# Attention and MLP on one core: where split rows live, when turned maxima are sent, and where the MLPs begin

## The chip, the cores and the metric

The kernel runs on one core of one Trainium2 chip. The metric is the time of one execution on the device in microseconds (us). A core has five engines that each work through a queue of their own in order: PE (matmul), DVE (vector), ACT (activation), POOL (general vector work) and SP, which here issues nearly all DMAs. They wait for each other through semaphores.

## The reference, cut to what matters

```python
# x: 2048 x 512; 32 heads of 16; F = 1792
qkv = layernorm(x) @ wqkv                    # q, k, v per head
p   = softmax(q @ k.T / 4)                   # per head, 2048 x 2048
h   = x + (p @ v, heads side by side) @ wo
out = h + silu(layernorm(h) @ w1) @ w2
```

## The kernel before

**Items and groups.** The attention is cut into 32 items of four heads by 512 query rows. Eight items make a block of 512 rows. An item has 16 groups, one for each 128 keys; group g belongs to item g // 16 and has place c = g % 16 in it, so there are 512 groups. In a group PE forms four scores tiles (`scores`: 64 rows of weights, because a head's 16 dimensions stand three times, as parts of a split number, beside 16 rows of constants and maxima), ACT takes the exponential of each (`pt<-ps`), and PE multiplies the weights of the group two before by the values (`values`, `LAG = 2`; in the trace eight matmuls `ps<-pt,va` for one group, since fp32 runs in two passes).

**Maxima.** Softmax subtracts each row's maximum, so for every item 64 further tiles of scores are formed ahead of it (`maximum`: a matmul `ps<-ks,qs` of 48 rows on PE and a reduction `mx<-ps` on DVE). The two kinds use opposite halves of PE's rows, so that a score and a maximum can run at the same time. `maxima(g)` is the planner: it says how many maxima group g takes, from the goals (`AHEAD`: how many groups before an item its maxima should be there) and from a list of `fixed` groups. `at["done"]` counts them.

When the last of an item's 64 maxima is there (`found_maxima`), they are reduced to one number per row and split (`finish_max`: one reduction on DVE and three small operations on POOL if urgent, otherwise nine small operations on POOL), and must stand in two rows of the tile `qs` before the item's first group. There are two ways. If there is time (more than `FAR` groups), `place_far` turns them on DVE (`mt<-ns`) `CALM` steps later, and one and two steps after that SP writes them to DRAM (`md<-mt`) and reads them back (`qs<-md`). If there is little time, `place_max` turns them on PE (`ps<-ident_h,ns`) `WAIT` steps later, DVE copies them (`mn<-ps`), and SP sends them (`qs<-mn`). One step is one group.

**Output and MLP of a block.** While the first item of the next block runs (items 8, 16 and 24, the constant `FIRSTS`), the block's rows are finished. Four tiles of 128 rows (t = 0 to 3): `split_rows` splits the attention's result into two f16 parts (tile `oh`, two buffers); in the groups c = 9 to 12 `output` runs the product with wo, 12 full matmuls each, and amid each product the number of maxima that `MORE` gives; DVE adds x and takes the statistics, `normalize` follows one group later, `split_normal` one more (ACT casts the high part, POOL or DVE subtracts; tile `g`, two buffers), and `turn_beside` transposes it by DMA into `hts` (`hts<-g`). From two groups after the first item, at the groups 146, 274 and 402, `beside_products` runs the MLP amid the attention, six half-matmuls in each group: first `first_of` (hidden units, `end_first` puts them into the tile `gates`), then `second_of`. Those groups are the set `beside`; I call the others plain.

**What sets the order.** The order on each engine is the order in which the code issues; `tick` runs what `soon` has put on the agenda for this step, before the group itself. Every item's accumulator is copied out by `finish_item` (`pvs<-ps`, on DVE for the first eight items and on ACT after).

Of the kernel before, what the change touches and what calls it, by code (L numbers as in the profile page):

```python
# [10 lines left out]
F32 = mybir.dt.float32  # L11
F32R = mybir.dt.float32r
F16 = mybir.dt.float16
# [7 lines left out]
P = 128  # L21
# [5 lines left out]
DC = D // P  # L27
FC = F // P
NB = S // 512
NG = 2 * D // P  # L30
KC = S // P
# [20 lines left out]
RING = 5  # L52
# [11 lines left out]
WAIT = 2  # L64
AHEAD = 6

JOINT = 2
MORE = 3, 3, 0, 0
FAR = 5
CALM = 3  # L70


OUTPUT = 8
# [1 line left out]
LOOK = 5  # L75

LEAD = 5


BESIDE_V = [(0, 0), (0, 0, 4, 4)], [(2, 4), (4, 4, 4, 4)], [(6, 6), (6, 6, 6, 6)]  # L80
# [9 lines left out]
def attention_mlp_kernel(ctx: ExitStack, tc: tile.TileContext, x, wqkv, wo, w1, w2, out):  # L90
# [35 lines left out]
    def dma(*a):  # L126
        pin(nc.sync.dma_start(*a))  # L127
# [157 lines left out]
    def start_of(piece):  # L285
        i, a = piece
        return KC * i + HALF * (a or 0)
# [26 lines left out]
    def finish_max(piece, urgent):  # L314

        m4 = mx.pop(piece).rearrange("p j a q k -> p (j a q) k")
        rows = m4.shape[1]
        nm = small.tile([P, 16], F32, name="nm")[:, :rows]
        sign = 1.0
        if urgent:  # L320
            pin(nc.vector.tensor_reduce(nm, m4, axis=AX.X, op=ALU.max, negate=True))
# [45 lines left out]
    def place_max(piece):  # L367

        i, a = piece
        ns = split.pop(piece)  # L370
        n = ns.shape[1]
        ps = bank("sm", F16)
        tr(ps[:n, :P], ns, ident_h)
        mt = small.tile([32, P], F16, name="mn", bufs=1)[:n]
        dve("tensor_copy", mt, ps[:n, :P])
        for j in range(2):
            dst = qs[i % RING][64 * j + 48:64 * j + 50, slice(None) if a is None else slice(a, a + 1)]
            dst = dst.rearrange("r a n -> r (a n)").rearrange("r (a b) -> r a b", b=P)
            dma(dst, mt[n // 2 * j:n // 2 * (j + 1), :])
        placed.add(piece)  # L380


    todo = {(i, j): sorted(((i, kb, qt, a, j) for kb in range(4) for a in range(2) for qt in range(4)),
# [6 lines left out]
    def soon(steps, fn, *a):  # L390

        agenda.setdefault(at["step"] + steps, []).append((fn, a))
# [15 lines left out]

    def found_maxima(piece):
        g = at["group"]  # L410
        if g is None or piece[1] is None and start_of(piece) - g > FAR:
            soon(WAIT + 1 if g is None else CALM, place_far, piece)
            finish_max(piece, False)
            return
        late.setdefault(at["step"] + WAIT, []).append(piece)
        unfinished.append(piece)
        found_at["step"] = at["step"]

# [43 lines left out]
    def weave(steps, inserts):  # L462

        for k, _ in enumerate(steps):
            if k + 1 in inserts:
# [4 lines left out]
    pts, den = {}, {}  # L470
    marks = [KC * (8 * b + 1) for b in range(1, NB)]

    beside = {g for m in marks for g in range(m + 2, min(groups, m + 2 + 4 * FC + 4 * FC))}
    fixed = {**{8 * KC * b + c: 3 + (MORE[c - OUTPUT - 1] if OUTPUT < c <= OUTPUT + 4 else 0) for b in range(1, NB) for c in range(2, KC + 2)},
             **{g: 4 for g in beside}}
    before = [sum(n for x, n in fixed.items() if x < g) for g in range(groups + 1)]
    free = [sum(x not in fixed for x in range(g)) for g in range(groups + 1)]
# [530 lines left out]
    def parts_of(w):  # L1008
        return w.bitcast(F16).rearrange("p (s n) -> p s n", s=2)
# [26 lines left out]

    def split_rows(b, t, chunks=slice(None)):
        if chunks.start != DC - 1:
            parts = zp.tile([P, 2, DC, P], F16, name="oh")
            os[t] = parts[:, 0], parts[:, 1]  # L1040
        (h, l), o = (x[:, chunks] for x in os[t]), ot[b % 2][:, t, chunks]
        if t > 1:
            act("copy", h, o)
        else:

            pool("tensor_copy", h, o)
        low(l, o, h, "pool")
# [26 lines left out]
    halves = {}  # L1074

    def split_normal(t):
        rows, halves[t] = hx.pop(t), parts_of(zp.tile([P, 512], F32, name="g"))
        act("copy", halves[t][:, 0], rows)
        low(halves[t][:, 1], rows, halves[t][:, 0], "pool" if t < 3 else "dve")

# [96 lines left out]

    def begin_mlp(b):
        chains.extend((3 * DC, 6, first_of(f), lambda ps, f=f: end_first(f, ps)) for f in range(FC))
        chains.extend((3 * FC, 7 if 4 * b + t == KC - 5 else 6, second_of(t), lambda ps, t=t: end_second(b, t, ps)) for t in range(4))  # L1180

    def half_product(j):
        if j == 0:
# [187 lines left out]
    def maxima(g):  # L1371

        i, c = divmod(g, KC)
        ready = at["ready"] = min(ITEMS, i + RING - (0 if c == KC - 1 else 1)) * 64
        late_now = at["step"] in late
        if g in beside:
            at["due"] = 0
            most = 4 - late_now + (64 + 4 * (g + (LEAD if g < marks[-1] else 3)) > at["done"])
            return max(0, min(most, ready - at["done"]))
        goals = [(64 * (n + 1), KC * n) for n in range(i + 1, LAST) if g >= FIRSTS[0] * KC or n <= FIRSTS[0] + 1]  # L1380
        goals += [(END - 32 * (1 - a), KC * LAST + HALF * a) for a in range(2) if g >= FIRSTS[0] * KC and KC * LAST + HALF * a > g]
        rate = 0
        for n, start in goals:
            end = max(g + 1, start - AHEAD)
            rate = max(rate, (n - (before[end] - before[g]) - at["done"]) / max(1, free[end] - free[g]))
        if g in fixed:
            rate = 3
        if ready < END:
            rate = min(rate, (ready - at["done"]) / (KC - 1 - c or KC))
        at["due"] += rate  # L1390
        if g < LAG:
            at["due"] = 0
            return 0
        most = 2 if late_now or c == JOINT and 0 < i <= FIRSTS[0] else 3 + (at["due"] >= 4 and i < FIRSTS[0])
# [116 lines left out]
```

## Time and profile before

| | us |
|---|---|
| median of 3 runs (1584.95 to 1586.16) | 1585.84 |
| the profiled execution | 1586.9 |
| its span on the core | 1585.1 |
| PE busy | 1561.1 |
| DVE busy | 1376.3 |
| ACT busy | 1234.7 |
| POOL busy | 573.6 |

The page says that the ends of matmuls are modelled, so that a busy PE is not PE at its peak: two matmuls on opposite halves of the rows count once, and so does one that runs alone. Stages are therefore compared by the time from one group's first value product to the next one's, with the granted clock (PEclk) beside it. The time outside the span is 1.8 us.

### The profile page before, as it was taken

How to read it: one execution, taken by the hardware profiler on the slowest of the kernel's cores; microseconds unless marked ns; L12 is line 12 of the kernel's file. 1: busy time of each engine (PE TensorE's matmuls, PEld its weight loads, DVE VectorE, ACT ScalarE, POOL GpSimd, SP SyncE). 2: the span in 40 equal slices, each digit the busy share in tenths (PEclk: the TensorE clock that was granted, in tenths of full speed). 3: DMA queues.
4: the chain of work that ended last, by engine and by line, in shares of the span. 5: the costliest groups of instructions: out<-in, count | busy, mean ns of one | idle time of the engine just before them, and what ended most of it. 6: DMA issues, size and time to landing. Idle time of an engine off the chain costs nothing.

```text
span 1585.1 us, 31197 instructions
## 1 busy us (share of the span) xinstructions
PE 1561.1 (98%) x11488; PEld 502.2 (32%) x11488; DVE 1376.3 (87%) x2202; ACT 1234.7 (78%) x2404; POOL 573.6 (36%) x843
## 2 busy tenths in 40 slices
PE   9999999999999999999999999999999999999999
PEld 6433222222222333333322333333322333332354
DVE  7999999999998999999988999999988999994322
ACT  6545799999977888888877888888867888878632
POOL 6643545454432545212242454302242445211100
PEclk9999999999999999999999999999999999999999
DMA  6667523334334122344433211444433221334332
GB/s 217 171 177 224 138 83 90 90 108 115 85 92 98 47 51 53 105 137 135 124 84 82 58 44 48 122 130 131 115 96 75 60 57 38 85 119 147 106 87 73
DMA packets 135554, 162.47 MB, mean 102 GB/s; under 512 B 42512, under 2 KB 79440, under 8 KB 135400
## 3 DMA queue, kind: packets, MB, share of 16 engines
q1 hardware_dynamic: 130648, 151.95, 34.6%
q10 hardware_dynamic: 4752, 8.52, 1.9%
q8 instruction: 90, 1.47, 0.4%
q14 instruction: 64, 0.52, 0.1%
HBM read 126.66 MB, written 24.81 MB: 96 GB/s over the span
## 4 chain that ended last, share of the span: by engine, by line
PE 84%; DVE 8%; ACT 3%; issue 1%; POOL 1%; DMA 1%; SPq 0%; ACTq 0%; POOLq 0%; DVEq 0%
PE ps L97 84%; DVE mx L307 5%; ACT pt L111 2%; DVE mx L305 1%; PE ps L100 1%; DMA hts<-g 0%; SPq L127 0%; ACT pvs L111 0%; DVE st L121 0%; POOL rs L104 0%; DMA ks<-in_A_x_dram 0%; ACT g L111 0%; POOL g L104 0%; POOL ri L104 0%; DVE w L121 0%
## 5 line engine op out<-in xcount | busy, mean ns | idle before, releaser
L307 DVE TENSOR_REDUCE mx<-ps 128x1 f32<-128x512 f32 x1842 | 1146.8, 683 | 77.7 <-PE ps L97 50.2
L111 ACT ACTIVATE pt<-ps 128x512 f32<-128x512 f32 x2048 | 1051.9, 606 | 195.3 <-PE ps L97 193.3
L97 PE MATMUL ps<-ks,qs 48*128 48x512 f16 x2048 | 678.6, 381 | 7.4 <-DVE mx L307 4.4
L97 PE MATMUL ps<-qs,ks 64*128 64x512 f16 x2048 | 643.6, 380 | 8.5 <-ACT pt L111 5.3
L97 PE MATMUL ps<-pt,va 128*17 128x512 f32 x4096 | 542.4, 602 | 0.5 <-DVE pvs L121 0.3
L97 PE MATMUL ps<-hts,w 64*128 64x512 f16 (+2 forms) x1212 | 285.0, 372 | 0.1
L97 PE MATMUL ps<-w,gates 64*128 64x512 f16 x1008 | 245.9, 378 | 0.9 <-ACT g L111 0.2
L97 PEld LDWEIGHTS <-ks 64*128 64x128 f16 x2048 | 176.8, 95 | 212.6 <-issue 167.1
L97 PEld LDWEIGHTS <-qs 48*128 48x128 f16 x2048 | 168.6, 94 | 71.6 <-issue 28.3
L97 PEld LDWEIGHTS <-w 64*128 64x128 f16 (+1 forms) x1212 | 101.7, 95 | 238.2 <-ACT pt L111 107.4
L104 POOL TENSOR_TENSOR ri<-rc,minus 128x16 f32<-128x16 f32 x31 | 90.7, 2926 | 179.9 <-DMA rc<-dn 179.7
L97 PEld LDWEIGHTS <-gates 64*128 64x128 f16 x1008 | 82.0, 94 | 219.3 <-ACT pt L111 120.4
L97 PEld LDWEIGHTS ps<-pt,va 128*17 128x17 f32 x4096 | 68.5, 95 | 214.3 <-issue 208.9
L305 DVE TENSOR_REDUCE mx<-ps 128x2 f32<-128x1024 f32 x103 | 119.3, 1218 | 4.1 <-PE ps L97 3.5
L104 POOL TENSOR_SCALAR t<-t,factors 128x512 f32<-128x512 f32 x42 | 29.0, 692 | 162.7 <-ACT t L111 162.7
L111 ACT ACTIVATE g<-ps,factors 128x512 f32<-128x512 f32 x68 | 47.0, 690 | 42.7 <-PE ps L97 42.7
L104 POOL TENSOR_TENSOR ot<-ot,g 128x512 f32<-128x512 f32 x12 | 15.2, 1268 | 164.9 <-ACT g L111 164.9
L104 POOL TENSOR_TENSOR mx<-mx 128x32 f32<-128x32 f32 x46 | 11.0, 239 | 153.0 <-DVE mx L307 146.7
L111 ACT ACTIVATE ks<-ps 128x512 f32<-128x512 f32 x30 | 17.9, 597 | 51.3 <-PE ps L97 46.0
L121 DVE SCALAR_TENSOR_TENSOR gh<-g,factors,gh 128x512 f16<-128x512 f32 x14 | 10.5, 752 | 52.1 <-ACT gh L111 52.1
L104 POOL TENSOR_TENSOR t<-t,g 128x512 f32<-128x512 f32 x42 | 53.6, 1276 | 3.5
L104 POOL TENSOR_TENSOR sl<-ks,sh 128x512 f16<-128x512 f32 x30 | 34.7, 1156 | 50.4 <-ACT sh L111 37.3
(161 smaller groups left out, 1062.1 us busy)
## 6 DMA issues: line engine op xcount, KB each, us to landing
w<-w2d SPq DMA_DIRECT2D x182, 256.0 KB
ks<-kd SPq DMA_DIRECT2D x120, 192.0 KB
w<-w1d SPq DMA_DIRECT2D x56, 256.0 KB
ks<-in_B_w_dram ACTq DMA_DIRECT2D x28, 256.0 KB
w<-in_B_w_dram SPq DMA_DIRECT2D x28, 256.0 KB
qs<-qd SPq DMA_DIRECT2D x128, 48.0 KB
kd<-sh SPq DMA_DIRECT2D x16, 256.0 KB
qd<-sh SPq DMA_DIRECT2D x16, 256.0 KB
```

Of the source, the lines that this page charges most:

```text
L97: return tc.keep_in_program_order(nc.tensor.matmul(*a, **k))
L100: tc.keep_in_program_order(nc.tensor.transpose(*a))
L104: tc.keep_in_program_order(getattr(nc.gpsimd, op)(*a, **k))
L111: ins = getattr(nc.scalar, fn)(*a, **k)
L121: pin(getattr(nc.vector, fn)(*a, **k))
L305: pin(nc.vector.tensor_reduce(of, space[:, n:n + 2, :], axis=AX.X, op=ALU.max))
L307: pin(nc.vector.tensor_reduce(of[:, j:j + 1], space[:, n, :], axis=AX.X, op=ALU.max))
```

## The change

- `split_rows` and `split_normal` no longer take a tile of their own with two buffers: they write into parts of `gates`, the tile of the hidden units, that no one uses at that time. The four tiles t then have four places.
- `MORE` gives three maxima amid each of the four output products, where the last two had none.
- `place_max` sends the turned maxima one step after it has turned them, no longer in the same step. In the items 8, 16 and 24 it turns them one step after they were found and no longer two, and the short way is taken there up to 8 groups ahead and not 5.
- `CALM` is 2, not 3, and on the far way the maxima found after group 128 are finished as urgent, so on DVE.
- The MLPs begin four groups after the item's first, not two (`BEHIND`). The second last of the last MLP's row tiles runs seven half-matmuls a group instead of six, as the last did.
- In the first eight items the planner aims at three groups ahead instead of six, and gives at least three maxima to each group.

```diff
-MORE = 3, 3, 0, 0
+MORE = 3, 3, 3, 3
-CALM = 3
+CALM = 2
+BEHIND = 4
... in place_max
-        for j in range(2):
-            dst = qs[i % RING][64 * j + 48:64 * j + 50, slice(None) if a is None else slice(a, a + 1)]
...
-        placed.add(piece)
+        def out():
+            for j in range(2):
+                dst = qs[i % RING][64 * j + 48:64 * j + 50, slice(None) if a is None else slice(a, a + 1)]
...
+            placed.add(piece)
+        soon(1, out)
... in found_maxima
-        if g is None or piece[1] is None and start_of(piece) - g > FAR:
+        output = g is not None and g // KC in FIRSTS
+        if g is None or piece[1] is None and start_of(piece) - g > FAR + 3 * output:
             soon(WAIT + 1 if g is None else CALM, place_far, piece)
-            finish_max(piece, False)
+            finish_max(piece, g is not None and g > FIRSTS[0] * KC)
             return
-        late.setdefault(at["step"] + WAIT, []).append(piece)
+        late.setdefault(at["step"] + (1 if output else WAIT), []).append(piece)
... the groups of the MLPs
-    beside = {g for m in marks for g in range(m + 2, min(groups, m + 2 + 4 * FC + 4 * FC))}
+    beside = {g for m in marks for g in range(m + BEHIND, min(groups, m + BEHIND + 8 * FC))}
... in split_rows
-            parts = zp.tile([P, 2, DC, P], F16, name="oh")
-            os[t] = parts[:, 0], parts[:, 1]
+            os[t] = [gates[:, t, m].rearrange("p (c n) -> p c n", n=P) for m in range(2)]
... in split_normal
-        rows, halves[t] = hx.pop(t), parts_of(zp.tile([P, 512], F32, name="g"))
+        rows, halves[t] = hx.pop(t), gates[:, FC - 4 + t]
... in begin_mlp
-        chains.extend((3 * FC, 7 if 4 * b + t == KC - 5 else 6, second_of(t), lambda ps, t=t: end_second(b, t, ps)) for t in range(4))
+        chains.extend((3 * FC, 7 if 4 * b + t in (KC - 6, KC - 5) else 6, second_of(t), lambda ps, t=t: end_second(b, t, ps)) for t in range(4))
... in maxima
-            most = 4 - late_now + (64 + 4 * (g + (LEAD if g < marks[-1] else 3)) > at["done"])
+            most = 4 - late_now + (64 + 4 * (g + LEAD) > at["done"])
-            end = max(g + 1, start - AHEAD)
+            end = max(g + 1, start - (AHEAD if g >= FIRSTS[0] * KC else 3))
-        if g in fixed:
-            rate = 3
+        if g in fixed or g < FIRSTS[0] * KC:
+            rate = 3 if g in fixed else max(rate, 3)
```

The order of the instructions shows it at three places (line numbers after the change are two higher).

**ACT while the second block's rows are split** (groups 267 to 274; `g` and `gates` are what `split_normal` writes, the names in brackets are the semaphores waited for, `DMAHW` those of DMAs). Before:

```order
L111 CAST oh<-ot_1881 128x512 [waits Pool_49]
L111 CAST g<-w 128x512 [waits DVE_49]
L111 ACTIVATE pt<-ps 128x512 [waits PE_49] x4
L111 CAST g<-w 128x512 [waits DVE_49]
L111 ACTIVATE pt<-ps 128x512 [waits PE_49] x4
L111 CAST g<-w 128x512 [waits DMAHW3_49,DVE_49]
L111 ACTIVATE pt<-ps 128x512 [waits PE_49] x4
L111 CAST g<-w 128x512 [waits DMAHW0_49,DVE_49]
L111 ACTIVATE pt<-ps 128x512 [waits PE_49] x12
L111 COPY pvs<-ps 128x512 [waits DMAHW4_49,PE_49]
```

and now:

```order
L113 CAST gates<-ot_1881 128x512
L113 CAST gates<-w 128x512 [waits DVE_49]
L113 ACTIVATE pt<-ps 128x512 [waits PE_49] x4
L113 CAST gates<-w 128x512 [waits DVE_49]
L113 ACTIVATE pt<-ps 128x512 [waits PE_49] x4
L113 CAST gates<-w 128x512 [waits DVE_49]
L113 ACTIVATE pt<-ps 128x512 [waits PE_49] x4
L113 CAST gates<-w 128x512 [waits DVE_49]
L113 ACTIVATE pt<-ps 128x512 [waits PE_49] x12
L113 COPY pvs<-ps 128x512 [waits DMAHW4_49,PE_49]
```

The casts of the third and fourth row tile no longer name a DMA among their waits; nothing moved.

**SP's DMAs at the end of item 8**, the last before item 9 begins (`w` are weights of the MLP, `dn` and `ot` belong to the item that has ended). Before:

```order
L131 DMA_TRANSPOSE hts<-g 128x8x128
L127 DMA md<-mt 32x32 x4
L127 DMA w<-w1d 128x1024
L131 DMA_TRANSPOSE hts<-g 128x8x128 x2
L127 DMA qs_108<-md 2x1024 x2
L127 DMA w<-w1d 128x1024
L127 DMA dn<-pvs 4x512
```

and now:

```order
L133 DMA_TRANSPOSE hts<-gates 128x8x128
L129 DMA qs_108<-mn 2x8x128 x2
L129 DMA w<-w1d 128x1024
L133 DMA_TRANSPOSE hts<-gates 128x8x128 x2
L129 DMA w<-w1d 128x1024
L129 DMA dn<-pvs 4x512
```

Item 9's maxima now go the short way, and stand ahead of the last two transposes instead of behind them. For the items 17 and 25 they went the short way already, between the first and the second transpose, and still do.

**DVE around the last two output products of the second block** (`ot<-ps` adds x to a product, `w<-ot` normalizes, `nm` and `mn` belong to the turned maxima). Before:

```order
L307 TENSOR_REDUCE mx<-ps 128x1 x3
L121 SCALAR_TENSOR_TENSOR ot_1881<-ps,factors,w 128x512
L121 TENSOR_SCALAR w<-ot_1881,mv,rs 128x512
L121 BN_STATS st<-ot_1881 128x6
L121 BN_AGGR mv<-st 128x2
L307 TENSOR_REDUCE mx<-ps 128x1
L321 TENSOR_REDUCE nm<-mx 128x16
L307 TENSOR_REDUCE mx<-ps 128x1 x2
L121 SCALAR_TENSOR_TENSOR ot_1881<-ps,factors,w 128x512
L121 TENSOR_SCALAR w<-ot_1881,mv,rs 128x512
L121 BN_STATS st<-ot_1881 128x6
L121 BN_AGGR mv<-st 128x2
```

and now:

```order
L309 TENSOR_REDUCE mx<-ps 128x1 x2
L323 TENSOR_REDUCE nm<-mx 128x16
L309 TENSOR_REDUCE mx<-ps 128x1 x4
L123 SCALAR_TENSOR_TENSOR ot_1881<-ps,factors,w 128x512
L123 TENSOR_SCALAR w<-ot_1881,mv,rs 128x512
L123 BN_STATS st<-ot_1881 128x6
L123 BN_AGGR mv<-st 128x2
L309 TENSOR_REDUCE mx<-ps 128x1 x2
L123 COPY mn<-ps 32x128
L309 TENSOR_REDUCE mx<-ps 128x1 x3
L123 SCALAR_TENSOR_TENSOR ot_1881<-ps,factors,w 128x512
L123 TENSOR_SCALAR w<-ot_1881,mv,rs 128x512
```

Between two additions of a product there are now six and five reductions where there were three and three, and the copy of the turned maxima comes one product earlier.

More of the change, by code (lines that the diff above doesn't have):

```diff
@@ L375, in place_max @@
         dve("tensor_copy", mt, ps[:n, :P])
-        for j in range(2):
-            dst = qs[i % RING][64 * j + 48:64 * j + 50, slice(None) if a is None else slice(a, a + 1)]
-            dst = dst.rearrange("r a n -> r (a n)").rearrange("r (a b) -> r a b", b=P)
-            dma(dst, mt[n // 2 * j:n // 2 * (j + 1), :])
-        placed.add(piece)
+        def out():
+            for j in range(2):
+                dst = qs[i % RING][64 * j + 48:64 * j + 50, slice(None) if a is None else slice(a, a + 1)]
+                dst = dst.rearrange("r a n -> r (a n)").rearrange("r (a b) -> r a b", b=P)
+                dma(dst, mt[n // 2 * j:n // 2 * (j + 1), :])
+            placed.add(piece)
+        soon(1, out)
     todo = {(i, j): sorted(((i, kb, qt, a, j) for kb in range(4) for a in range(2) for qt in range(4)),
@@ L471, in attention_mlp_kernel @@
     marks = [KC * (8 * b + 1) for b in range(1, NB)]
-    beside = {g for m in marks for g in range(m + 2, min(groups, m + 2 + 4 * FC + 4 * FC))}
-    fixed = {**{8 * KC * b + c: 3 + (MORE[c - OUTPUT - 1] if OUTPUT < c <= OUTPUT + 4 else 0) for b in range(1, NB) for c in range(2, KC + 2)},
+    beside = {g for m in marks for g in range(m + BEHIND, min(groups, m + BEHIND + 8 * FC))}
+    fixed = {**{8 * KC * b + c: 3 + (MORE[c - OUTPUT - 1] if OUTPUT < c <= OUTPUT + 4 else 0) for b in range(1, NB) for c in range(BEHIND, KC + BEHIND)},
              **{g: 4 for g in beside}}
```

## The prediction

> **What bounds the kernel now.** I read the page's busy times and chain first, then stretches of one or a few groups, then the waits in the few groups that stand out.
>
> ```profile
> PE 1561.1 (98%) x11488; PEld 502.2 (32%) x11488; DVE 1376.3 (87%) x2202; ACT 1234.7 (78%) x2404; POOL 573.6 (36%) x843
> PE 84%; DVE 8%; ACT 3%; issue 1%; POOL 1%; DMA 1%; SPq 0%; ACTq 0%; POOLq 0%; DVEq 0%
> ```
>
> PE is busy nearly always and carries 84% of the chain, but that does not say what one more maximum costs. The stretches do. First a plain group with three maxima, then one with four and the group behind it; then an MLP group with four maxima and seven with five; two that hold three and five; six with six half-matmuls and no maxima, and five with seven. Columns: length, then busy PE, PEld, DVE, ACT and POOL, PEclk, DMA share, GB/s.
>
> ```profile
> 237.91:239.87 1.96, 1.96 (x17) 0.44 (x16) 1.89 (x4) 1.96 (x6) 1.81 (x3) 1.00 0.15 55
> 239.87:242.36 2.49, 2.33 (x18) 0.53 (x17) 2.42 (x5) 2.49 (x7) 0.65 (x1) 1.00 0.01 3
> 242.36:244.37 2.01, 2.01 (x17) 0.44 (x16) 2.00 (x4) 1.58 (x4) 0.00 (x0) 1.00 0.03 8
> 573.43:576.04 2.61, 2.61 (x25) 0.85 (x23) 2.48 (x5) 2.04 (x5) 2.47 (x3) 1.00 0.02 6
> 844.43:866.05 21.62, 21.04 (x163) 6.57 (x162) 21.58 (x36) 15.54 (x31) 7.42 (x8) 1.00 0.41 96
> 1357.89:1363.63 5.74, 5.67 (x48) 1.73 (x46) 5.06 (x10) 4.58 (x10) 0.42 (x2) 1.00 0.15 49
> 1440.90:1456.34 15.44, 14.84 (x112) 3.81 (x110) 5.89 (x13) 12.94 (x26) 0.64 (x3) 1.00 0.26 87
> 1461.80:1474.93 13.13, 13.13 (x97) 3.61 (x96) 0.00 (x0) 10.31 (x21) 5.45 (x6) 1.00 0.65 217
> ```
>
> A plain group takes 1.96 us with ACT full; a fourth maximum costs 2.49 + 2.01 - 2 x 1.96 = 0.58. An MLP group takes 2.61 with four maxima and 21.62 / 7 = 3.09 with five, DVE full. Without maxima it takes 15.44 / 6 = 2.57, and with seven half-matmuls 13.13 / 5 = 2.63.
>
> The second thing is three holes, the three groups at the start of the items 9, 17 and 25. The second one also stands group by group.
>
> ```profile
> 483.68:496.26 12.58, 9.79 (x54) 2.10 (x54) 7.50 (x13) 7.62 (x16) 0.00 (x0) 0.73 0.29 62
> 831.46:844.43 12.97, 10.47 (x54) 2.17 (x53) 7.81 (x13) 8.86 (x17) 0.00 (x0) 0.74 0.47 101
> 1185.65:1199.01 13.36, 10.88 (x55) 2.16 (x54) 7.82 (x13) 8.77 (x17) 0.00 (x0) 0.74 0.45 100
> ...
> 831.46:837.45 5.99, 3.56 (x17) 0.63 (x16) 3.48 (x6) 4.13 (x8) 0.00 (x0) 0.78 0.90 182
> 837.45:841.11 3.66, 3.66 (x17) 0.59 (x16) 1.95 (x4) 1.89 (x5) 0.00 (x0) 0.50 0.16 58
> ```
>
> The last of each three is an MLP group with five maxima. At the prices above they would take 1.96 + 1.96 + 3.09 = 7.01; the holes are 5.57, 5.96 and 6.35, together 17.9 us. The clock falls to 0.50 in the group behind the wait. Why PE waits, in time order, first in item 9, then in item 17 (SPq is SP issuing DMAs):
>
> ```profile
> 479.11 1.71 SPq L127 DMA_DIRECT2D md<-mt  x4
> 482.35 2.87 SPq L131 DMA_TRANSPOSE hts<-g  x2
> 485.40 0.59 SPq L127 DMA_DIRECT2D qs<-md  x2
> 487.45 0.60 PE L97 MATMUL ps<-qs,ks 64*128 64x512 f16 x1 [2.72 <-DMA qs<-md]
> ...
> 828.66 1.39 SPq L127 DMA_DIRECT2D qs<-mn  x2
> 830.16 1.26 SPq L131 DMA_TRANSPOSE hts<-g  x1
> 832.15 3.77 SPq L131 DMA_TRANSPOSE hts<-g  x2
> 833.32 0.62 ACT L111 CAST g<-w 128x512 f16<-128x512 f32 x1 [2.22 <-DMA hts<-g]
> 834.49 0.37 PE L97 MATMUL ps<-qs,ks 64*128 64x512 f16 x1 [1.97 <-ACT pt L111]
> ```
>
> In item 9 the maxima's way back stands on SP behind two transposes; PE waits 2.72 us. In item 17 the transpose stands behind the maxima's DMAs; the cast of the fourth row tile waits 2.22 us for the transpose that still reads its buffer, the exponentials stand behind that cast on ACT, and PE waits for them.
>
> **The change part by part.**
>
> *The holes.* With a place for each row tile the cast waits only for DVE, as ACT's order shows. In item 9 the short way stands ahead of the last two transposes. Its time, from the same steps in item 17: the short way's issue begins 828.66 - 825.16 = 3.5 us after the third group before the item (rows below) and ends at 4.9; from the end of the issue at 485.99 to PE's start at 487.45 it is 1.46, so the rows are there at 6.35. The item's scores would start after three groups (6.30) and the 1.05 us from a group's beginning to its scores (487.45 - 2.72 - 483.68), at 7.35. That leaves 1.0 us. The other items get theirs a product earlier. The MLP's first product needs the last transpose; before, it was issued by 832.15 + 3.77 = 835.92 although its cast came at 833.32. Four groups behind, it has some 7.8 us from the item's start (4 x 1.96), so no wait comes there. I take all: -17.9, bounds -17.9 and -9.
>
> The cold clock belongs to this term. After idle gaps of 1.97 and 2.72 us the stretch behind runs at 0.50, with 1.00 in every other stretch above. [...]
>
> *Maxima moved.* Counted in PE's order: of plain groups, 13 fall from four maxima to three in the first eight items, three with three come in and one with two (2.0) goes: -13 x 0.58 + 3 x 1.96 - 2.0 = -3.7. Of MLP groups, one with five goes (3.09), five with three (5.74 - 3.09 = 2.65), one with two (2.6) and seven with none (2.57); nine with seven half-matmuls and none (2.63) and three with seven and four maxima come. The trace has none of these last: between 2.63 and 3.09; 2.85, since they add one half-matmul to the four-maxima group, nearest to the middle. Sum -36.9 + 32.2 = -4.7. Together -8.4. The last MLP still ends with the last group, so nothing behind it moves.
>
> *Output products.*
>
> ```profile
> 804.80:810.18 5.38, 5.35 (x32) 1.63 (x31) 4.77 (x9) 3.47 (x8) 2.64 (x5) 1.00 0.58 157
> 810.18:815.68 5.50, 5.47 (x31) 1.63 (x30) 5.32 (x10) 2.56 (x5) 1.89 (x3) 1.00 0.49 114
> 820.42:825.16 4.74, 4.71 (x29) 1.61 (x28) 4.39 (x8) 2.56 (x5) 3.31 (x8) 1.00 0.37 76
> 825.16:831.46 6.30, 6.30 (x46) 1.43 (x45) 5.53 (x11) 4.54 (x9) 2.69 (x4) 1.00 0.25 63
> 476.80:483.68 6.88, 6.87 (x47) 1.31 (x46) 6.51 (x13) 5.47 (x12) 2.68 (x4) 1.00 0.60 132
> ...
> 825.32 0.75 DVE L121 SCALAR_TENSOR_TENSOR ot<-ps,factors,w 128x512 f32<-128x512 f32 x1 [0.32 <-issue]
> 827.26 1.26 DVE L307 TENSOR_REDUCE mx<-ps 128x1 f32<-128x512 f32 x2
> ...
> L307 DVE TENSOR_REDUCE mx<-ps 128x1 f32<-128x512 f32 x1842 | 1146.8, 683 | 77.7 <-PE ps L97 50.2
> ```
>
> The first two products with six maxima take 5.38 and 5.50, the last two with three 4.74. There DVE also normalizes: from the addition to the first reduction it is 1.94 us, and six reductions at 1146.8 / 1842 = 0.62 make 3.7. So DVE sets 5.65, which I take. Four such groups cost 0.91 each; two with five maxima and the turn come to some 5.45, 0.7 each: +5.0 (bounds 4 x 0.64 + 2 x 0.5 = 3.6 by the first row's 5.38, 6.6 by 0.3 more each).
>
> *The three groups behind them.* They took 6.30 with eight maxima and 6.88 with nine. The first block goes from nine to eight, the others from eight to nine: -0.6 + 1.2. The casts (0.62) and DVE's subtraction for the last row tile then fall into full groups, no longer into the hole: some 0.5 in each block. +2.1 (0 to 4).
>
> *Two more plain groups at an item's start.* ACT copies the accumulator out there (`pvs`). The nearest rows are the start of item 16, where ACT is full:
>
> ```profile
> 790.17:792.87 2.70, 2.02 (x17) 0.55 (x16) 1.59 (x4) 2.70 (x7) 1.83 (x3) 1.00 0.00 0
> 792.87:795.00 2.13, 2.13 (x16) 0.44 (x16) 2.13 (x5) 2.13 (x6) 0.80 (x1) 1.00 0.13 24
> ```
>
> 0.74 + 0.17 = 0.91 above two plain groups. Items 9, 17 and 25 get it, items 16 and 24 lose it, being MLP groups now: +0.9.
>
> *An added wait: `CALM`.* Counted in DVE's order, the turn (`mt`) came six to eight reductions after an item's last one; now three to five in the items 3 to 8. The fence shows the steps of item 3, then an urgent item's reduction, then the two groups in which item 11 went the long way.
>
> ```profile
> 206.65 0.24 POOL L104 TENSOR_TENSOR mx<-mx 128x32 f32<-128x32 f32 x1 [7.48 <-DVE mx L307]
> 209.28 0.22 POOL L104 TENSOR_TENSOR ns<-nm,ns 128x16 f16<-128x16 f32 x1
> 210.41 0.20 DVE L121 STREAM_TRANSPOSE mt<-ns 128x32 f16<-128x32 f16 x1
> ...
> 823.60 0.21 DVE L321 TENSOR_REDUCE nm<-mx 128x16 f32<-128x64 f32 x1
> 568.20:573.43 5.23, 5.23 (x47) 1.70 (x45) 4.94 (x9) 5.19 (x12) 2.41 (x4) 1.00 0.22 53
> ```
>
> POOL's nine steps take 209.50 - 206.65 = 2.85 us; DVE came 0.91 later. Three reductions of a plain group last 1.96 and four 2.6, so DVE waits 0.9 twice and 0.25 twice, with its later reductions and then PE's maxima behind it: 2.3 at most, 0 if PE's banks hide it; +1.0. Later items need three steps on POOL in place of nine, and their four reductions last 2.6: nothing. Their reduction on DVE (0.21) falls into groups where DVE is idle for 2.61 - 2.48 = 0.13; the rest is paid back in the next group: nothing, at most 16 x 0.1. The items 18 and 26 to 30 change from the short way to the long one, with 1.71 + 0.59 us of issue on SP for 1.39; item 11's two groups with the same DMAs took 5.23, so 2.61 each: nothing.
>
> *The writes into `gates`* wait for the last MLP's reads of the same parts. In PE's order these stand 11 or more groups before, so they cost nothing.
>
> *Sum*: -17.9 - 8.4 + 5.0 + 2.1 + 0.9 + 1.0 = -17.3. The profiled execution of 1586.9 would take 1569.6; the median, 1.06 lower, 1568.5.
>
> **Rivals.**
>
> 1. DVE takes the hole over: it has no idle time from the third product to the item's start, the fourth tile's normalization, then ACT's cast, then the exponentials come late. Against it: in the row of 6.30 DVE is busy for 5.53. Half the hole back: +9, 1577.5.
> 2. The added maxima hide behind PE better than I say (+3.6, 0, 0.9, 0): 1564, five less. For it: DVE's first product row has 0.6 idle.
> [...]
> 4. The change does not do what it says: the casts wait in another way, and 17.9 stays: 1586. ACT's order speaks against it.
> 5. The other side: the turned maxima miss the start of the items. Sent one group later, they have 1.0 us in item 9; SP could hold them if the weights' load or the transpose ahead waits. Late by 6 us in each block, it costs 6 + 1.7 for the cold group: 3 x 7.7 - 17.3 = +5.8, 1591.6. It decides from about 4 us late in all three (4 + 1.7 = 17.3 / 3); the items 17 and 25 have over 5 us more room.
>
> **How the numbers follow.** A difference under 0.2% (3.2 us) is about what a measurement cannot tell from none. Forecast 0.62, rival 1 0.13, 2 0.12, 3 0.05, 4 0.03, 5 0.05. Faster is 0.92 (forecast and 1 to 3), same 0.03, slower 0.05. The forecast's own range, by its bounds, is 1564 to 1574; to take in rival 2 and half of rival 1 I give 1562 to 1577.
>
> **What would show it.** Right: no wait of ACT for `hts`, none of PE for `qs` at the items 9, 17 and 25; PEclk 1.00 there; three groups in about 6 us; last products at 5.4 to 5.7; no row with 2.49 in most of items 0 to 7. Wrong: a PE wait above 1 us at an item's or the MLP's start, product groups above 6, or DVE idle before `mt`.

## The result, and the profile after

The changed kernel takes 1571.98 us (median of 4 runs, 1571.37 to 1572.08), the kernel before 1586.0 on the same chip; the ratio is 0.9911, interval 0.9894 to 0.9928. On another chip it took 1571.67 against 1586.54, ratio 0.9907, interval 0.9890 to 0.9923. So 14 to 15 us are gone, where 17.3 were forecast. The forecast of 1568.5 is 3.5 us too low; the time lies within the range. The profiled execution has a span of 1569.6 us, 15.5 less than before.

First the page, its busy times and its chain:

```profile
PE 1553.5 (99%) x11484; PEld 501.1 (32%) x11484; DVE 1377.7 (88%) x2216; ACT 1233.6 (79%) x2404; POOL 552.7 (35%) x759
PE 87%; DVE 9%; ACT 2%; issue 1%; POOL 0%; DMA 0%; POOLq 0%; ACTq 0%; DVEq 0%
```

PE's busy time fell by 7.6 us, the span by twice that: half was waiting, half busy time (a cold clock counts as busy: the group that stood at a clock of 0.50 was busy for all of its 3.66 us). POOL does 84 operations fewer, since maxima after group 128 are finished on DVE. Then the stretches that answer to those of before (columns as there):

```profile
294.85:297.80 2.95, 2.94 (x16) 0.52 (x16) 2.56 (x6) 2.95 (x7) 2.71 (x6) 1.00 0.21 78
461.56:467.28 5.72, 5.52 (x32) 1.64 (x31) 5.68 (x11) 3.08 (x6) 2.41 (x4) 1.00 0.00 0
467.28:472.99 5.71, 5.51 (x31) 1.63 (x30) 5.55 (x12) 2.56 (x5) 2.71 (x7) 1.00 0.65 113
472.99:479.30 6.31, 6.31 (x47) 1.39 (x46) 5.70 (x12) 4.90 (x11) 2.33 (x4) 1.00 0.35 69
479.30:486.53 7.23, 7.07 (x47) 1.39 (x46) 6.77 (x11) 6.66 (x15) 0.00 (x0) 1.00 0.59 137
486.53:488.80 2.27, 2.17 (x15) 0.45 (x16) 2.11 (x5) 2.27 (x6) 0.00 (x0) 1.00 0.09 17
488.80:492.55 3.75, 3.10 (x25) 1.09 (x24) 2.71 (x5) 2.98 (x7) 0.00 (x0) 1.00 0.20 33
811.89:817.73 5.84, 5.51 (x31) 1.64 (x30) 5.80 (x12) 3.08 (x6) 2.87 (x7) 1.00 0.00 0
817.73:823.11 5.38, 5.29 (x32) 1.63 (x31) 4.83 (x11) 2.56 (x5) 2.70 (x4) 1.00 0.26 50
823.11:830.97 7.86, 7.72 (x47) 1.39 (x46) 7.83 (x14) 6.45 (x13) 1.91 (x3) 1.00 0.68 161
830.97:837.37 6.40, 6.38 (x47) 1.32 (x46) 6.11 (x11) 5.36 (x12) 0.00 (x0) 1.00 0.36 82
833.36:835.32 1.96, 1.96 (x16) 0.44 (x16) 1.74 (x4) 1.63 (x5) 0.00 (x0) 1.00 0.54 146
1178.17:1184.57 6.40, 6.38 (x47) 1.31 (x46) 6.10 (x11) 5.36 (x12) 0.00 (x0) 1.00 0.39 85
```

The holes are nearly closed. The three groups at the start of the items 9, 17 and 25 are all plain now, 3 x 1.96 = 5.88, and take 7.23, 6.40 and 6.40: 2.4 us of hole where 17.9 stood. PEclk is 1.00, and the group that stood at 3.66 with a clock of 0.50 takes 1.96. The last two output products take 5.72 and 5.71 in the first block, with six maxima each, and 5.84 and 5.38 in the second, with six and five. The three groups behind the products take 6.31 and 7.86. One of four long plain groups in the first eight items stands at 294.85 (the others take 2.29, 2.29 and 2.94); longer than 1.96 are also the last plain group ahead of the MLP (2.27) and the first MLP group (3.75 for 3.09).

What is left in item 17 shows in time order, ACT, DVE and POOL first, then SP for the items 9 and 17:

```profile
826.44 0.64 ACT L113 CAST gates<-w 128x512 f16<-128x512 f32 x1
...
827.10 1.50 DVE L123 TENSOR_SCALAR w<-ot,mv,rs 128x512 f32<-128x512 f32 x1
827.16 1.16 POOL L106 TENSOR_TENSOR gates<-w,gates 128x512 f16<-128x512 f32 x1 [0.82 <-ACT gates L113]
...
828.87 0.68 ACT L113 CAST gates<-w 128x512 f16<-128x512 f32 x1
```

```profile
476.50 1.41 SPq L129 DMA_DIRECT2D qs<-mn  x2
...
478.46 2.96 SPq L133 DMA_TRANSPOSE hts<-gates  x2
...
821.24 1.41 SPq L129 DMA_DIRECT2D qs<-mn  x2
...
823.66 1.27 SPq L133 DMA_TRANSPOSE hts<-gates  x1
```

The casts have no wait behind them. In item 17 the maxima's DMAs leave at 821.24, ahead of the fourth product's end at 823.11; before, at 828.66, 3.5 us behind it. So the transpose behind them leaves earlier too. In item 9 (the first two lines) they stand ahead of the last two transposes. But DVE's normalization of the fourth row tile takes 1.50 us, where the other tiles' take 0.53 to 0.54.

In the experiments, "row r" is the stretch that begins with the values of group r, and scores run three groups ahead: in row 141 the scores of item 9 begin, in 269 and 397 those of the items 17 and 25.

### The profile page after: what moved, and what is told of

Read it like the earlier page. It is cut to its first block, busy times and chain, and to the rows that moved or that the text cites. A ratio compares the mean times of both kernels' runs of the same rounds, so it can differ in the third digit from the quotient of the medians.

```text
span 1569.6 us, 31094 instructions
## 1 busy us (share of the span) xinstructions
PE 1553.5 (99%) x11484; PEld 501.1 (32%) x11484; DVE 1377.7 (88%) x2216; ACT 1233.6 (79%) x2404; POOL 552.7 (35%) x759
## 4 chain that ended last, share of the span: by engine, by line
PE 87%; DVE 9%; ACT 2%; issue 1%; POOL 0%; DMA 0%; POOLq 0%; ACTq 0%; DVEq 0%
PE ps L99 87%; DVE mx L309 6%; ACT pt L113 2%; DVE mx L307 1%; PE ps L102 1%; DVE st L123 0%; DVE w L123 0%; DVE pvs L123 0%; DVE ot L123 0%; DVE ks L123 0%; POOL wv_l L106 0%; DMA ks<-in_A_x_dram 0%; POOL rs L106 0%; ACT g L113 0%; DVE mv L123 0%
## 5 line engine op out<-in xcount | busy, mean ns | idle before, releaser
L99 PEld LDWEIGHTS <-gates 64*128 64x128 f16 (+1 forms) x1152 | 95.1, 94 | 240.3 <-ACT pt L113 112.8
L106 POOL TENSOR_TENSOR ot<-ot,g 128x512 f32<-128x512 f32 x12 | 15.3, 1271 | 128.5 <-ACT g L113 128.5
L113 ACT ACTIVATE ks<-ps 128x512 f32<-128x512 f32 x30 | 17.9, 597 | 51.7 <-PE ps L99 46.3
L106 POOL TENSOR_TENSOR gates<-t,gates 128x512 f16<-128x512 f32 x42 | 48.6, 1158 | 3.4
```

Of the source, the lines that this page charges most:

```text
L99: return tc.keep_in_program_order(nc.tensor.matmul(*a, **k))
L106: tc.keep_in_program_order(getattr(nc.gpsimd, op)(*a, **k))
L113: ins = getattr(nc.scalar, fn)(*a, **k)
```

## The experiments

The first four are the places alone, the change without them, the MLPs' start, and `MORE`.

**The places alone, on the kernel before.**

```diff
-            parts = zp.tile([P, 2, DC, P], F16, name="oh")
-            os[t] = parts[:, 0], parts[:, 1]
+            os[t] = [gates[:, t, m].rearrange("p (c n) -> p c n", n=P) for m in range(2)]
-        rows, halves[t] = hx.pop(t), parts_of(zp.tile([P, 512], F32, name="g"))
+        rows, halves[t] = hx.pop(t), gates[:, FC - 4 + t]
```

> The kernel before with one part of the change, the places in gates for split_rows and split_normal. Theory (the prediction's): the holes of the items 17 and 25 come from ACT's casts that wait for transposes, so they close to what is left after the whole change (2.4 us of row where it was 6, the cold group behind at 1.96 instead of 3.66), with some 1 us given back in the groups ahead; item 9's hole comes from SP's queue and stays at 5 to 6 us of row. Time 1586.0 - 2 x (3.6 + 1.7 - 1.0) = 1577.4, 1575 to 1580. Rival A, the casts are not the cause: 1586, all three holes stay. Rival B, the casts cause item 9's hole too: all three close, 1573.

Measured: 1577.78 against 1586.63, ratio 0.9945 (0.9928 to 0.9962). The three stretches of the prediction, in this kernel:

```profile
483.66:495.08 11.42, 8.58 (x54) 1.93 (x53) 7.50 (x13) 7.62 (x16) 0.00 (x0) 0.85 0.32 68
830.32:839.17 8.85, 8.13 (x55) 2.04 (x54) 7.82 (x13) 7.99 (x17) 0.00 (x0) 1.00 0.66 148
1180.85:1189.70 8.85, 8.12 (x54) 2.04 (x54) 7.81 (x13) 7.99 (x17) 0.00 (x0) 1.00 0.66 150
```

The second and third fell by 4.1 and 4.5 us and are no longer cold; the first stays open, with a wait of PE for `qs<-md` (2.77 us). The theory holds as it was put: the casts made the holes of the items 17 and 25, and SP's queue that of item 9.

**The change without the places** (the same edit backwards, on the changed kernel).

> The changed kernel with this one part undone (the tiles oh and g with two buffers each). Theory: the casts wait for transposes again in the items 17 and 25, and now in item 9 too, since there the short way was the cure for SP's queue alone: each hole gives 3 to 5 us back, a cold group returns, 1572 + 3 x 4 = 1584, 1580 to 1587. Rival: the short way and the four groups behind closed the holes, and the places add nothing: 1572, no wait of ACT for a transpose.

Measured: 1571.87, the time of the changed kernel, and its rows but for two (0.28 us each). The theory failed. A part that is worth 9 us on the kernel before is worth nothing beside the rest of the change.

**The MLPs two groups behind again.**

```diff
-BEHIND = 4
+BEHIND = 2
-        ... 7 if 4 * b + t in (KC - 6, KC - 5) else 6 ...
+        ... 7 if 4 * b + t == KC - 5 else 6 ...
```

> The changed kernel with the MLPs two groups behind, as before (and six half-matmuls in the second last of the last MLP's row tiles, so that the groups suffice). Theory (phase): ACT's work at the end of a hidden tile falls beside the copy of the accumulator again at the items' ends (place 15 of the first MLP stage), 3.02 us for 2.61, nine or ten times, +3.7 to +4; the mix of groups is +0.3 at the prices; the transposes are issued by 832.3 and landed by 835, as early as the MLP then begins, so no wait is added: 1574 to 1576.5. Rival A (room for the transposes): PE waits at the MLP's first products, 1 to 3 us in each block, 1575 to 1581, and the rows at place 15 stay at 2.61. Rival B: neither matters, 1572.

Measured: 1574.02 (1573.89 to 1574.03), 2.0 more. All nine rows at place 15 of the first MLP stage go from 2.61 to 3.02, +3.7. One of them with ACT's work in it:

```profile
533.59:536.61 3.02, 2.97 (x24) 0.84 (x24) 2.83 (x6) 3.02 (x8) 0.00 (x0) 1.00 0.00 0
```

```profile
533.60 0.69 ACT L113 ACTIVATE g<-ps,factors 128x512 f32<-128x512 f32 x1
534.17 1.10 ACT L113 ACTIVATE pt<-ps 128x512 f32<-128x512 f32 x2
535.13 0.62 ACT L113 COPY pvs<-ps 128x512 f32<-128x512 f32 x1
535.59 2.13 ACT L113 ACTIVATE pt<-ps 128x512 f32<-128x512 f32 x4
```

ACT has the end of a hidden tile and the copy of the accumulator in one group and is full for 3.02 us. A hidden tile takes four groups (its 12 half-matmuls on each side, six in a group, the sides in turn), so a start two groups later puts the two into different groups. No wait for a transpose appears. The 3.7 is partly offset: the rows 268 and 269 take 5.00 together instead of 5.60 and the rows 396 and 397 4.96, and the start of the MLP costs less.

**`MORE` as before.** `MORE = 3, 3, 0, 0` on the changed kernel.

> The changed kernel with MORE = 3, 3, 0, 0: no maxima added amid the last two products. Theory: 18 maxima move from groups of products (0.3 each) into MLP groups (17 more with five at 3.09, 19 fewer with four at 2.61): at the prices +9.0 - 4.6 = +4.5; the three groups behind the products lose the 2 to 2.6 us that the added maxima brought there: 1574 to 1576.5. Rival: the whole wave of DVE's work behind the products comes from the added maxima, and with it the rest of the holes (3.2, 2.4 and 2.4 us of row): these fall to 1.96 and the time stays at 1572 or falls.

Measured: 1577.41 (1576.09 to 1577.64), 5.4 more, above both theories. In the trace's rows it is +4.3: 2.1 from the products, the groups behind them and the other groups together, and 2.2 from a longer wait in item 9 (row 141, 5.42 for 3.22), which no theory had:

```profile
476.66 2.66 SPq L133 DMA_TRANSPOSE hts<-gates  x2
479.38 1.41 SPq L129 DMA_DIRECT2D qs<-mn  x2
```

```profile
PE ps L99 <- DMA qs<-mn: 3.4, 1, 3.4
```

Without the six maxima the DMAs of item 9's maxima stand behind the last two transposes. In the changed kernel they stand ahead of both. So `MORE` closes item 9's hole as well. The short way alone does not: with the planner's part alone (below) item 9's maxima go that way too, and PE waits 3.99 us for them. Whether the short way is needed beside `MORE`, no run shows.

The next follow what these left: the long groups of the first eight items, the long normalization, and the places that were not needed.

**`CALM` 3 in the first eight items.**

```diff
-            soon(WAIT + 1 if g is None else CALM, place_far, piece)
+            soon(WAIT + 1 if g is None else CALM + (g < FIRSTS[0] * KC), place_far, piece)
```

> The changed kernel with CALM 3 instead of 2 while g < 128, so that the far turn of the items 3 to 8 stands one group later on DVE. Theory: DVE waits at the turn for POOL's nine small operations and PE for DVE's reductions behind it; with three reductions more ahead the wait is gone: the four groups 36, 57, 100 and 121 go from 2.29, 2.95, 2.29 and 2.94 us to 1.96, so 1572.0 - 2.6 = 1569.4 (1569 to 1570). Rival: these groups are long for another reason (an item's last maximum, a load), the excess stays or moves one group on: 1572.

Measured: 1569.24 (1568.99 to 1569.43). All four groups are back at 1.96. What DVE did in the group at 294.85 of the changed kernel, POOL's last step and the turn:

```profile
294.99 0.22 POOL L106 TENSOR_TENSOR ns<-nm,ns 128x16 f16<-128x16 f32 x1
```

```profile
295.25 0.21 DVE L123 STREAM_TRANSPOSE mt<-ns 128x32 f16<-128x32 f16 x1 [0.98 <-POOL ns L106]
```

DVE waits 0.98, and PE's group is 0.99 longer: PE's banks hide nothing. The price of the other side is small: item 8's maxima are sent a group later, and row 125 waits for `qs<-md` for some 0.1 us (0.4 to 0.6 in the later variants).

**The subtractions for the third and fourth tile change engines.**

```diff
-        low(halves[t][:, 1], rows, halves[t][:, 0], "pool" if t < 3 else "dve")
+        low(halves[t][:, 1], rows, halves[t][:, 0], "pool" if t != 2 else "dve")
```

> The changed kernel with the subtraction for the third row tile on DVE and that for the fourth on POOL (before it was the other way round): DVE and POOL do as many of them as before. Theory: in the items 17 and 25 DVE's normalization of the fourth tile lasts 1.50 and 1.49 us instead of 0.53 because it begins together with POOL's subtraction of the third (1.16 us), so the two exclude each other; with POOL free there it takes 0.53 again, and in item 9 the 0.74 us that DVE stood idle ahead of the last subtraction go: -0.96 - 0.96 - 0.7 = -2.6, 1569.4 (1569 to 1570.5). Rival A: the normalization is long for another reason (its input, PE's banks): it stays at 1.5, 1571.5 to 1572. Rival B: the subtraction, now earlier on DVE, waits for ACT's cast and holds up the reductions: slower, 1572.5 to 1574.

Measured: 1569.99 (1569.80 to 1570.04), 1.7 to 2.0 less than the changed kernel. DVE in item 17:

```profile
827.07 0.69 DVE L123 TENSOR_TENSOR gates<-w,gates 128x512 f16<-128x512 f32 x1
827.68 0.54 DVE L123 TENSOR_SCALAR w<-ot,mv,rs 128x512 f32<-128x512 f32 x1
828.13 3.08 DVE L309 TENSOR_REDUCE mx<-ps 128x1 f32<-128x512 f32 x5
```

With POOL idle beside it the same normalization takes 0.54, and rival A falls. The rows 268 and 269 together go from 5.60 to 4.83, as do 396 and 397: 0.77 each. Item 9 gave nothing: 0.52 of DVE's idle time there is a wait for ACT's cast, and it only moved to the third tile's subtraction.

**Both.**

> The changed kernel with both of these edits (CALM 3 while g < 128, and the third tile's subtraction on DVE, the fourth's on POOL). Theory: they touch different groups and add up, 1572.0 - 2.6 - 2.6 = 1566.8 (1566 to 1568.5). Rival: one of them gives nothing: 1569.4.

Measured: 1567.69 (1567.44 to 1567.99), 4.0 to 4.3 less than the changed kernel; the parts gave 2.4 to 2.7 and 1.7 to 2.0. They add up.

**Without the places, and the turn as before.** On the kernel without the places, `place_max` sends in the same step, and `late` is `at["step"] + WAIT` everywhere.

> The changed kernel without the places, and with place_max as before (turned two steps after the maxima were found in the output's items too, and sent in the same step). Without the places alone nothing changed (1571.87). Theory: the holes of the items 17 and 25 have two conditions, a cast that needs its buffer and a transpose that stands on SP behind the maxima's DMAs; the places take away the first, the earlier turn the second, and each is enough. With both undone the casts wait for transposes again: rows of 5.5 to 6 us at 269 and 397 and cold rows of 3.66 behind, some 3.7 more in each of the two blocks, and 0 to 4 in item 9, where the turn comes a group later: 1580 (1578 to 1584). Rival: what closed them is the MLPs' later start or the maxima amid the products, 1572 to 1574 with no wait of ACT for a transpose.

Measured: 1580.14 (1579.14 to 1581.07), 8.3 more than without the places alone. Item 17, SP, then ACT, then the stretches:

```profile
827.57 1.41 SPq L129 DMA_DIRECT2D qs<-mn  x2
829.07 1.26 SPq L133 DMA_TRANSPOSE hts<-g  x1
```

```profile
832.23 0.62 ACT L113 CAST g<-w 128x512 f16<-128x512 f32 x1 [2.23 <-DMA hts<-g]
```

```profile
830.36:836.36 6.00, 3.56 (x16) 0.62 (x16) 3.48 (x6) 4.04 (x8) 0.00 (x0) 0.86 0.87 178
836.36:840.02 3.66, 3.66 (x16) 0.59 (x16) 1.95 (x4) 1.88 (x5) 0.00 (x0) 0.50 0.17 63
```

The hole of before is back to 0.1 us, with its cold group; the MLPs' later start and `MORE` were both in this kernel and did not close it. In item 9 row 141 is as long as in the changed kernel (3.23 for 3.22), though PE now waits 0.97 us for `qs` in it.

**The places, and the turn as before**, the fourth corner.

> The changed kernel with place_max alone as before (turned two steps after the maxima were found in the output's items too, and sent in the same step), the places kept. Theory (either the places or the early turn is enough for the items 17 and 25): no wait of ACT for a transpose, no cold group, rows 269 and 397 at 2.4 to 3.3 us, 1571.5 to 1573.5. Rival (the early turn is what closes them): 1578 to 1580, as with both undone (1580.14).

Measured: 1570.78 (1570.56 to 1571.10), beside 1571.67 for the changed kernel on the same chip. There is no wait of ACT for a transpose and no cold group, rows 269 and 397 are at 3.23, and the time is 0.9 us less. So each of the two is enough, and with the places the early turn costs something. In this kernel POOL's subtraction begins after the normalization and not beside it, which then takes 0.53, and the rows 267 to 269 take 7.8 us together instead of 8.3. In item 9 PE waits 0.97 us for `qs`, as in the run before, but row 141 is hardly longer for it (3.24 for 3.22).

**The planner's part for the first eight items alone, on the kernel before.**

```diff
-            end = max(g + 1, start - AHEAD)
+            end = max(g + 1, start - (AHEAD if g >= FIRSTS[0] * KC else 3))
-        if g in fixed:
-            rate = 3
+        if g in fixed or g < FIRSTS[0] * KC:
+            rate = 3 if g in fixed else max(rate, 3)
```

> The kernel before with the planner's part for the first eight items alone (three groups ahead instead of six, at least three maxima in each group; CALM, MORE and the rest as before). Theory: the number of maxima is fixed, so what leaves the plain groups (12 fewer with four, 11 more with three: -8 us with their neighbours) comes back in MLP groups (16 more with five, 18 fewer with four, one more with one: +8 to +9): 1586.5 + 0 to 1.5, so 1586.5 to 1588. Rival (the plain groups' gain stands for itself, the prediction's -3.7): 1582 to 1583.

Measured: 1586.76 against 1586.54, ratio 1.0002 (0.9993 to 1.0012). The first eight items with the groups up to the first product, and the MLP's groups 145 to 167, in this kernel and before:

```profile
180.72:449.23 268.51, 266.89 (x2011) 59.31 (x2011) 256.68 (x416) 264.95 (x539) 128.74 (x190) 1.00 0.38 104
492.35:560.61 68.26, 66.62 (x522) 20.92 (x521) 65.51 (x109) 53.65 (x105) 26.80 (x31) 1.00 0.24 63
```

```profile
180.68:456.44 275.76, 272.06 (x2024) 60.10 (x2023) 263.55 (x428) 266.94 (x539) 128.39 (x190) 1.00 0.37 102
499.35:560.33 60.98, 60.93 (x508) 19.38 (x507) 57.46 (x94) 53.18 (x105) 28.25 (x37) 1.00 0.27 72
```

-7.3 us here, +7.3 there. The number of maxima is fixed: taking them out of plain groups gains nothing if MLP groups must take them.

**A better version**: `CALM` as above, and

```diff
-        low(halves[t][:, 1], rows, halves[t][:, 0], "pool" if t < 3 else "dve")
+        low(halves[t][:, 1], rows, halves[t][:, 0], "dve" if b and t == 2 else "pool")
```

> The changed kernel with CALM 3 while g < 128, the fourth tile's subtraction on POOL in each block, and the third's on DVE in the second and third block alone. Theory: in the first block DVE stood idle for 0.52 us ahead of the third's subtraction, waiting for ACT's cast, and worked 0.69 on it, so 1.2 less than with the third on DVE everywhere (1567.69): 1566.5 (1566 to 1567). Rival (DVE is not what holds PE there): 1567.7.

Measured: 1567.07 (1566.91 to 1567.36) against 1586.54, ratio 0.9878 (0.9861 to 0.9894), 4.6 less than the changed kernel on the same chip. The first block's rows 140 and 141 fell from 5.43 (in the run with both) to 4.71, 0.7 of the 1.2 expected: DVE now waits 0.22 us for PE there, so it is no longer all that holds PE. This beats both kernels.

**The changed kernel again**, for that comparison.

> The changed kernel again, on the same chip as the others of this call: 1571.5 to 1572.5, so that a difference of 1 us between the calls is known for what it is.

Measured: 1571.67 (1571.58 to 1571.78).

## Why the prediction was right, and where it was off

The direction and the mechanism were right; the sum was 2.0 us too low in the traces' rows (-15.3 for -17.3). The rest of the 3.5 is mostly how the two profiled executions stand in their runs: that of before was above its median, that of after (1571.37) below. That the sum missed by so little is partly luck: the first five terms of the table came out 6.9 us too low together, and 4.9 of it was made up by an effect that was not seen (-3.7) and by the maxima, of which not all is assigned (-1.2).

| term | forecast | measured | where |
|---|---|---|---|
| holes | -17.9 | -15.5 | 1.35, 0.52, 0.52 left |
| output products | +5.0 | +5.4 | 2 x 0.97 in the first block, 1.10 + 0.64 in the others |
| three groups behind them | +2.1 | +2.55 | -0.57, +1.56, +1.55 |
| plain groups at an item's start | +0.9 | +2.9 | 0.31 + 0.66 at each MLP's start |
| `CALM` | +1.0 | +2.6 | 0.33 and 0.99, twice each |
| place 15 in the first MLP stage | not seen | -3.7 | nine rows, 0.41 each |
| maxima moved | -8.4 | -9.6 | by difference |

*The holes.* Both conditions stand in the prediction: a cast that needs its buffer, and a transpose that stands behind the maxima's DMAs. Only the first was credited, and "with a place for each row tile the cast waits only for DVE" is true but was not needed here. The four corners (places and early turn 1571.67 to 1571.98, early turn alone 1571.87, places alone 1570.78, neither 1580.14, each with the rest of the change) show that each is enough. Of item 9 the step was right that its maxima must leave SP ahead of the last transposes; what brings them there is `MORE`, as the run without it shows.

*The 2.4 that stayed* was the failed step "I take all". In item 9 it is DVE, which waits 0.74 us there for ACT's cast of the fourth tile and then works 0.69 on the subtraction; with that subtraction on POOL (the better version) the rows 140 and 141 lose 0.76 of the 1.35. In the items 17 and 25 it is the normalization beside POOL's subtraction (1.50 and 1.49 us for 0.53), shown by the run that moved the subtraction (269 and 397 are at 1.96 there, 268 and 396 at 2.87). Such a pair stood in the trace of before, unread; POOL first, then DVE:

```profile
820.85 1.16 POOL L104 TENSOR_TENSOR g<-w,g 128x512 f16<-128x512 f32 x1
```

```profile
821.25 1.04 DVE L121 TENSOR_SCALAR w<-ot,mv,rs 128x512 f32<-128x512 f32 x1
```

It ends 0.28 us after POOL's operation (820.85 + 1.16 = 822.01, 822.29). In the changed kernel the normalization does so too (827.16 + 1.16 = 828.32, 828.60), though it is recorded to begin 0.06 earlier. DVE's reductions `mx<-ps` are not lengthened beside POOL (0.68 us on average in both cases). What makes the one operation wait for the other, no run shows.

*The cold clock* was rightly put to the waits: it went where the wait went (the places alone, 1.00 in the items 17 and 25), stayed in item 9 there (0.85), and came back with the wait (neither, 0.50). Rival 3, that the cold groups stay though the waits go, had no support: no group of the changed kernel's attention is cold.

*Plain groups at an item's start.* The wrong row: the 0.91 that I read at item 16 as the cost of the copy did not vanish when those two groups became MLP groups. It moved two groups on (rows 257 and 258, 2.70 and 2.13), and went again with the MLPs two groups behind. It belongs to the passage from MLP to plain groups. Two terms of -0.9 were credited for nothing. At the MLP's start 0.97 more come in each block, and the copy explains only a part. The copy delays ACT, and the group ahead takes 2.27. But most of the first MLP group's excess (3.75 for 3.09) comes without the copy: with the MLPs two groups behind, PE's wait of 0.51 us in that group ends with exponentials that ACT does ahead of the copy, and the group still takes 3.65. In the kernel before, such an excess stood inside the holes (the first MLP groups took 3.32 to 3.73), whose third group the prediction priced at 3.09.

*`CALM`* was sized between 0 and 2.3, and 2.6 came, a little above the upper bound. Nothing in the trace spoke for banks that hide a wait of DVE. A wait of DVE ahead of `mt` was named as a sign of being wrong, and it came (0.98 us).

*Place 15* was the omission. The two groups' delay was read for the transposes' room alone, which the changed kernel does not need: with the start two groups behind no such wait came. What it changes is which of ACT's operations meet in one group. Rows of 3.02 among those of 2.61 stood in the trace of before, three in each block, 16 groups apart.

*Maxima moved and output products* belong together. Alone, the planner's part gives -7.3 and +7.3. The gain is that 16 more maxima go under products than before; the run without them puts it at 2.1 us, and item 9's hole comes on top. Of -9.6, 0.6 comes from the first eight items (-8.1 without `CALM`'s wait for 13 x 0.58); the rest of the difference isn't assigned.

Rival 1 happened in small: DVE does hold PE at the item's start, at a quarter of its price (2.4 of 9). Rival 2 did not: the added maxima cost what was said. Rival 5 did not: no group of the changed kernel waits for `qs`, though the run without `MORE` (3.39 us) and the two with the turn as before (0.97) show how near it is.

Three slips in the prediction change none of this. The upper bound of the output products adds up to 6.8 and not 6.6. The range of 1564 to 1574 "by its bounds" leaves out the holes' bound of -9; with it the bounds reach some 1582. And the sign "no row with 2.49 in most of items 0 to 7" contradicts the count of 13: one such row stays in each of the items 1 to 7 (groups 16, 32 and so on to 112).

## What to carry to other kernels

When a wait has two conditions, ask of every edit in the change whether it takes away one of them; credit the sum once, and expect that undoing either edit shows nothing. A shift by some groups moves not only due times but also which operations of another engine meet in one group: look for a row that is longer at a regular distance, and work out where the shift puts it. Where an engine that feeds the bound waits in order, take the whole wait as the price unless a row shows slack, and where one DVE operation is two or three times as long as its twins (1.04 and 1.50 us for 0.53 here), look at what POOL does in that moment.

## What was not expected of the hardware

The clock does not go by the length of the gap alone. Nine traced gaps of 1.94 to 3.99 us were each followed by a group of 3.1 to 3.7 us with a mean clock of 0.50 to 0.60 (three before, one with the places alone, two with neither, three with the planner's part alone). In the run without `MORE` PE waited 3.39 us (5.42 - 2.03), and neither this stretch nor the group behind it (1.95 us) shows a cold clock:

```profile
477.56:482.98 5.42, 2.03 (x17) 0.44 (x16) 2.81 (x5) 2.30 (x6) 0.00 (x0) 1.00 0.66 146
```

The nine cold stretches last 3.41 us (three) or 6.83 us (six), once or twice 3.41. In the kernel before they begin at 486.65, 834.81 and 1189.79, so 348.16 and 354.98 us apart, which is 102 and 104 times 3.413. My estimate from these numbers is that the clock changes only at the ends of windows of 3.41 us, and goes down where PE was busy for too little of the window that ends there. In item 9 of the kernel before, that window and the cold stretch are:

```profile
483.24:486.65 3.41, 1.49 (x10) 0.14 (x9) 2.49 (x4) 1.97 (x4) 0.00 (x0) 1.00 0.81 156
486.65:493.48 6.83, 6.03 (x26) 1.17 (x30) 3.58 (x6) 3.80 (x8) 0.00 (x0) 0.50 0.14 38
```

ahead of the cold stretches of the items 17 and 25 the window is

```profile
831.40:834.81 3.41, 1.44 (x10) 0.32 (x10) 0.84 (x2) 1.49 (x4) 0.00 (x0) 1.00 1.05 219
1186.38:1189.79 3.41, 0.99 (x7) 0.28 (x4) 1.65 (x3) 2.30 (x5) 0.00 (x0) 1.00 0.85 183
```

and in the run without `MORE` the two windows across which the wait falls:

```profile
476.89:480.30 3.41, 1.72 (x15) 0.25 (x11) 2.49 (x4) 2.41 (x5) 0.00 (x0) 1.00 0.73 139
480.30:483.72 3.42, 1.72 (x15) 0.44 (x15) 1.26 (x3) 1.30 (x3) 0.00 (x0) 1.00 0.33 94
```

Ahead of the three cold stretches PE was busy for 0.44, 0.42 and 0.29 of the window (1.49 / 3.41 = 0.44); the wait of 3.39 us is split, and each of its windows is 0.50 busy. No other window of the attention in the traces of before and after, counted from a recorded change of the clock, is below 0.79. So a gap of 2 us inside one window was followed by a cold group (1.97 us in item 17, 1.96 in item 25), and one of 3.4 us across two was not. No run was made to test this, the ends of PE's busy times are modelled, and at the end of one program (the two subtractions exchanged) a window of 0.46 was not followed by a cold one, so the limit is not known exactly. The other three runs of the kernel without `MORE` took 1.2 to 1.6 us more than this one, near the 1.7 of a cold group, so the windows may fall otherwise in them; no trace of those shows it.

DVE's normalization and POOL's subtraction lengthen each other, in both directions. POOL's subtraction of 1.16 us takes 1.48 where it begins during a normalization (at 480.85 in the kernel before), and the normalization of 0.53 takes 0.69 to 1.50, by how much of POOL's operation is still ahead: in all six such pairs in the traces of before and after it ends 0.28 us after POOL's operation, whether it is recorded to begin 0.06 us ahead of it or 0.76 behind.
